# The second batch of a strided-attention and softplus kernel: one TensorE visit a pair, masks added by VectorE, and another order for the first chunk

## The chip, the cores and the metric

The kernel runs on one core of a Trainium2 chip. A core has TensorE (PE, matrix products; its weight loads are listed as PEld), VectorE (DVE), ScalarE (ACT), GpSimd (POOL) and SyncE (SP, which issues most transfers). Each engine works through its own queue in order and waits on semaphores for the others. The metric is device time in microseconds, as the median of several runs; lower is better.

## The reference

```
scores = scale * q @ k^T                      # 8 batches, 8 heads, 576 positions, 64 per head
heads 0 to 3: keep 0 <= i - j < 32            # local
heads 4 to 7: keep i >= j with i % 32 == j % 32   # strided
attn = softmax(masked scores);  x = attn @ v  # x becomes 4608 rows of 512
h = x @ w_in                                  # 512 -> 2048
g = max(h, 0) + log1p(exp(-|h|))              # softplus
out = g @ w_out                               # 2048 -> 512
```

Everything is float32 in the result. The kernel keeps that accuracy by splitting each operand of the large products into a high and a low part and adding three products: high by high, high by low, low by high.

## The kernel before, in words

Two heads make a pair, so each batch has four pairs, numbered `n` from 0 to 31 over the batches; with 8 batches, pairs 0 to 3 are batch 0 and 4 to 7 are batch 1. For strided heads the positions are regrouped by class, so that both kinds of mask leave only 64 keys to a block of 32 queries. A pair's scores then fill 9 chunks of 64 columns: `part` 0 holds six of them and `part` 1 three.

The feed-forward part runs over 9 chunks `c` of 512 rows, each in 16 steps `f` over the hidden width. A step `F` (`hidden`, 12 products of 512 columns into a `ph` bank, of which there are two) makes the hidden values; ScalarE turns them into `u` in three activations (`A`, `Ae`, `Al`), VectorE finishes the softplus (`u`), its high and low halves (`Gh`, `Gl`) are made, and a step `O` (`output`, 12 products) adds them to four `py` banks.

The attention of a pair has these steps, named by a letter and the pair: `q`, `k`, `v` (loads), `D` (lays the queries out for both heads, one half each), `S` (scores), `X` (maxima), `x` or `s` (scales the maxima into a bias), `E` (exponentials, with their sums), `r` and `R` (guard and reciprocal), `M` (normalizes), then the transposition of the probabilities: `T` on TensorE with a copy `C` for batch 0, `P` on VectorE for later ones (16 instructions in a block). `V` makes the weighted sums in two halves, and `H` and `L` put their high and low parts into `x`. The weights pass through `w` (load), `a` (ScalarE), `B` and `d` (VectorE), `h` and `l` (high and low half), for `i` and `o`, 16 tiles each, all during the first chunk.

Two things set the order. For the first chunk it is written out by hand: the string `FIRST` lists some 550 steps, and the lists `ON_POOL`, `ON_VECTOR` and `ON_SCALAR` move single steps from their usual engine. From the second chunk on a small planner (`Plan`, lines 79 to 115) places the steps from given costs and due times. In that planned part one visit of TensorE makes both score parts of pair `n` and the sums of pair `n-1`:

```
        def work(i=i, n=n):
            scores(n, 0)
            scores(n, 1)
            if joint(i):
                sums_of(n - 1)
```

The scores there carry no mask when they leave TensorE; VectorE adds it on the way to SBUF (`add_mask`). In batches 0 and 1 TensorE itself adds the mask, as a product of an identity with the mask table (`add` in `scores`, line 340). In batch 1 the score parts are separate steps `S40`, `S41` and so on, and each half of the sums is one too (`V40`, `V41`). The dictionary `shared` keeps the `po` bank whose upper columns hold part 1 of a pair's scores, and whose lower ones later take a half of the sums of the pair before. In batch 0 both halves of the sums use the one `po` bank, except for pair 3. The wait for a bank to come free is set by the `H` and `L` that read it.

`zeros(n)` clears the query buffer's unused blocks: for pairs 0 to 3 and for the buffer `qT` that all later pairs share.

Of the kernel before, what the change touches and what calls it, by code (L numbers as in the profile page):

```python
# [18 lines left out]
P = 128  # L19
# [13 lines left out]


FIRST = """
W mask q0 D00 k0 D01 S00 X00 Y00 q1 D11 S01 X01 E00 x01 Z00 k1 D10 S11 X11 q2 D20 Y11 E01 r0 wi0
S10 X10 D21 x10 k2 S21 ai0 wo0 q3 D31 S20 R0 M0 E10 Bi0 di0 X21 hi0 E11 T00 x21 C00 ao0 Z11 r1
X20 T01 C01 Bo0 D30 v0 R1 do0 V00 H00 T02 C02 L00 Y20 M1 k3 S31 X31 E21 E20 Z20 V01 li0 wi1
S30 H01 L01 ai1 Bi1 r2 di1 x31 R2 M2 wi3 ai3 T10 C10 T11 C11 v1 T12 ho0 lo0 Bi3 V10 T21 X30 Y30
di3 C12 H10 L10 V11 E30 T20 E31 Z30 C21 H11 v2 L11 r3 R3 M3 C20 T22 wi2 ai2 Bi2 V20 C22  # L40
H20 L20 di2 hi3 li3 T32 k4 wo1 C32 wi9 T31 ao1 T30 C31 v3 C30 hi1 li1 V21 H21 wo2 ao2 L21 V31 wi4
V30 Bo1 Bo2 ai9 H31 L31 Fa0 q4 H30 L30 F0 wi10 do1 Bi9 di9 wo3 Fa1 hi2 li2 D4 S40 A0
Ae0 Al0 ho1 lo1 ao3 F1 u0 Gh0 X40 x40 F2 Bo3 Gl0 ai4 Bi4 hi9 li9 di4 do2 ho2 v4 A1 E40 S41
X41 x41 wi5 ai5 q5 Bi5 Ae1 Al1 u1 wo15 D5 lo2 O0 wi6 hi4 di5 li4 F3 Gh1 Gl1 O1 A2 Ae2 wi8 ai8
do3 ai10 k5 E41 S50 r4 hi5 wo12 Bi8 li5 Al2 A3 di8 u2 R4 Ae3 M4 Al3 wi7 ai7 wi12 hi8 X50
x50 F4 u3 Gh3 Bi10 di10 F5 Gh2 Gl2 wo5 wo4 ho3 lo3 E50 P4 O2 A4 Gl3 q6 hi10 ao5 Bo5 Ae4 Al4
u4 wi11 S51 A5 Ae5 li8 X51 li10 ai6 Al5 Bi7 di7 V40 H40 x51 Gh4 Gl4 E51 r5 F8 hi7 do5 u5 ao4
L40 O3 D6 Bi6 A8 Ae8 Al8 wi14 V41 H41 Bo4 li7 di6 do4 ho4 hi6 R5 M5 k6 wo6 lo4 Gh5 S60
u8 Gh8 X60 F7 ao6 ho5 x60 E60 Gl5 li6 F6 A6 O4 ai11 L41 P5 wo7 ao7 wo8 Gl8 A7 Bo6 do6 Bo7 Ae6 Al6
v5 V50 H50 S61 Ae7 Al7 lo5 O5 ho6 u6 Gh6 Bi11 L50 do7 X61 x61 ai12 Bi12 F9 lo6 q7 wo9 D7 Gl6  # L50
V51 di12 E61 di11 H51 L51 ho7 k7 S70 X70 u7 lo7 hi11 li11 r6 k8 A9 O6 ao9 Bo9 x70
Gh7 Ae9 Gl7 ao8 F11 do9 Bo8 do8 Al9 u9 wi13 ai13 Bi13 di13 hi12 li12 wi15 ho8 lo8 wo10
ao10 Bo10 O7 R6 M6 A11 do10 hi13 F10 O8 ho10 Ae11 Al11 Gh9 u11 Gh11 ho9 lo9 F12 Gl9 O9
lo10 P6 wo11 A10 Ae10 Al10 u10 ao11 Bo11 ao12 E70 S71 ai15 do11 Bi15 v6 V60 q8 Gl11 A12 Ae12
li13 F13 Gh10 H60 X71 L60 ai14 Bo12 V61 k9 Gl10 wo14 di15 H61 Al12 do12 L61 u12 Bi14 O10 wo13
ho11 lo11 di14 A13 Ae13 Al13 u13 Qa0 x71 E71 r7 hi14 R7 O11 li14 Gh13 F14 ho12 lo12 Gh12
Gl12 O12 Gl13 A14 Ae14 Al14 M7 P7 u14 hi15 li15 ao13 Bo13 ao14 do13 ao15 v7 V70 ho13 H70 F15
A15 L70 V71 H71 lo13 Bo14 do14 ho14 lo14 O13 Ae15 L71 v8 Al15 u15 Gh15 Q1 Gh14 Gl14 O14 Bo15
do15 D8 Q0 QA1 Gl15 Qu1 QA0 Qu0 ho15 lo15 O15 Qh0 y0 Ob15 q9 y1 Qh1 Ql0 y2 y3 Ql1
"""  # L60

ON_POOL = """
D10 D20 x10 D31 hi0 x21 r2 x31 r3 hi3 hi1 ho1 Gh0 ho2 x41 hi4 r4 x50 x51 x60 Gh6 x61 r6 ho8 ho10
ho9 x71 r7 hi14 hi15 ho13 ho14 ho15
""".split()
ON_VECTOR = """
D01 M0 C00 M3 li3 li1 li2 lo1 Gl0 li9 lo2 li4 Gl1 Gl4 li6 lo6 Gl6 lo7 Gl7 li12 lo8 M6 Gl9 lo11
li14 M7 lo13 Gl14 Gl15
""".split()
ON_SCALAR = """  # L70
y1 y3
""".split()

WIDE = """
# [44 lines left out]
def attention_softplus_ffn(  # L119
# [95 lines left out]
    taken = []  # L215
    phs, us, ghs, gls = {}, {}, {}, {}

    def zeros(n):

        for h in range(2):  # L220
            to = blocks_of(n)[64 - 64 * h : P - 64 * h, :, h]
            (nc.vector if n < 2 else nc.gpsimd).memset(to, 0.0)
        if n < NPAIR:
            nc.gpsimd.memset(k_of(n)[:, :PAD], 0.0)

# [95 lines left out]

    def scores(n, part):

        b = order[n][0]
        masked = b < 2
        if b == 0:
            ps = py[2 * (n % 2) + part]
        elif b == 1 or part == 0:
            taken.append(n)
            ps = ps_s.tile([P, 512], F32, tag="ps", name=f"ps_{n}_{part}")  # L330
        else:
            shared[n] = ps_o.tile([P, 512], F32, tag="po", name=f"po_{n}")
# [14 lines left out]


        if masked and n > 0:
            add(True)  # L350
        for x in range(lo, hi):
            for place in range(2):
                a, i = block_at(x, place)
                c = TILE * a + 32 * i
                nc.tensor.matmul(  # L355
                    ps[rows[place], 64 * (x - lo) : 64 * (x - lo) + 64],
                    lhsT=blocks_of(n)[:, c // 32].rearrange("p h l -> p (h l)"),
                    rhs=k_of(n)[:, c : c + 64],
                    start=not masked or n == 0 and x == lo,
                    stop=not masked or n > 0 and x == hi - 1,  # L360
                )
        if masked and n == 0:
            add(False)
# [65 lines left out]
    def row_exp(n):  # L429
        pv, _, _ = parts(n)  # L430
        nc.scalar.activation(pv, pv, AF.Exp, scale=SCALE)

    def row_sums(n):
        pv, _, (_, sm, _, _) = parts(n)
        nc.vector.tensor_reduce(sm, pv, axis=AX.X, op=ALU.add)
# [72 lines left out]
    def weighted(n, half, joint=False):  # L508


        if joint:
            if half == 0:
                po = shared[n + 1]
            else:
                po = ps_h.tile([P, 512], F32, tag="ph", name=f"pv_{n}")
        elif half == 1 and (n == NPAIR - 1 or n >= 2 * NPAIR):
            taken.append(n)
            po = ps_s.tile([P, 512], F32, tag="ps", name=f"pv_{n}_{half}")
        else:
            po = ps_o.tile([P, 512], F32, tag="po", name=f"pv_{n}_{half}")  # L520
        pos[n, half] = po
        for x in range(NTILE // 2):
            a = NTILE // 2 * half + x
            for h in range(2):
                nc.tensor.matmul(  # L525
                    po[64 * h : 64 * h + 64, TILE * x : TILE * x + TILE],
                    lhsT=vs[n][:, a, h, :],
                    rhs=pt_of(n, a)[:, h, a % 2],
                    start=True,
                    stop=True,  # L530
                )
# [170 lines left out]
    def of(name, usual):  # L702
# [3 lines left out]
                return engine  # L706
        return usual

    first["mask"] = lambda: nc.scalar.dma_start(mask_b, masks)
    first["W"] = lambda: dummies(10)  # L710
    for n in range(2 * NPAIR + 2):
        task(f"q{n}", load_q, n)
        task(f"k{n}", load_k, n)
        if n > 2 * NPAIR:
            continue
        task(f"v{n}", load_v, n)
        if n < NPAIR:
            for h in range(2):
                task(f"D{n}{h}", lay_out_q, n, (h,), of(f"D{n}{h}", nc.scalar))
        else:  # L720
            task(f"D{n}", lay_out_q, n)
        if n >= 2 * NPAIR:
            continue
        for j in range(2):
            task(f"S{n}{j}", scores, n, j)
            task(f"X{n}{j}", maxima, n, j)
            if f"{n}{j}" in WIDE:
                task(f"Y{n}{j}", subtract, n, j)
                task(f"E{n}{j}", wide_exp, n, j)
                task(f"Z{n}{j}", sums, n, j)  # L730
            else:
                task(f"x{n}{j}", bias_of, n, j, of(f"x{n}{j}", nc.vector))
                task(f"E{n}{j}", exponentials, n, j)
# [3 lines left out]
        if f"P{n}" in FIRST.split():  # L737
            task(f"P{n}", prob_transposes, n)
        else:
            for g in range(3):  # L740
                task(f"T{n}{g}", early_transposes, n, g)
                task(f"C{n}{g}", early_copy, n, g, of(f"C{n}{g}", nc.scalar))
        for half in range(2):
            task(f"V{n}{half}", weighted, n, half)
# [255 lines left out]
```

## Time and profile before

| | us |
|---|---|
| median of 3 runs | 890.61 (890.55 to 891.92) |
| span of the profiled execution | 890.1 |
| TensorE busy | 879.0 |
| VectorE busy | 576.6 |
| ScalarE busy | 445.8 |
| GpSimd busy | 64.0 |

The page gives the profiled execution by its span from the first to the last instruction; the span is 0.5 below the median of the runs. Groups are named by line, engine, operation, and output and input tile. L629 and L669 are the products of `F` and `O`; L355 are the scores, L340 the mask products, L525 the sums, L495 and L477 the transposes on TensorE. L641, L644 and L646 are the three activations of a step, L650, L662 and L264 its softplus and halves (L264 is the line of every plain copy). A table by stretch gives, for each stretch of the span, the busy time of every engine and the number of its instructions.

### The profile page before, as it was taken

The page shows a single profiled execution, that of the slowest core. Times are in us where ns is not written, and L with a number is a line of the kernel's source. Part 1 is how long each engine was busy: PE and PEld are TensorE (multiplying, and loading weights), DVE is VectorE, ACT ScalarE, POOL GpSimd, SP SyncE. Part 2 cuts the span into 40 slices and gives each one's busy share as a digit, 9 for nine tenths or more (in the row PEclk, how much of TensorE's full clock was granted, in tenths as well). Part 3 has the DMA queues.
Part 4 walks back from the last instruction along what each step waited for, and adds up shares of the span by engine and source line. Part 5 has one row for each costly group of instructions (what it writes and reads, how often), then busy time and mean ns, then how long its engine had stood idle before and what let it go on. Part 6 is the DMA issues. An engine that isn't in the chain of part 4 may idle for free.

```text
span 890.1 us, 14332 instructions
## 1 busy us (share of the span) xinstructions
PE 879.0 (99%) x5634; PEld 723.6 (81%) x5634; DVE 576.6 (65%) x1268; ACT 445.8 (50%) x796; POOL 64.0 (7%) x93
## 2 busy tenths in 40 slices
PE   7999999999999999999999999999999999999998
PEld 5778888888888888888888888888888888888886
DVE  7878877788766777776766676677777333333332
ACT  7999665554544445445445454445543333333332
POOL 7254350000000000000000000000000000000000
PEclk9999999999999999999999999999999999999999
DMA  9856202121211122111211121111200010001001
GB/s 337 314 205 209 93 18 76 56 75 45 91 37 30 36 74 62 44 45 32 92 44 45 44 92 30 30 43 54 81 18 18 1 48 1 0 1 48 1 1 48
DMA packets 50083, 58.27 MB, mean 65 GB/s; under 512 B 3168, under 2 KB 35296, under 8 KB 50016
## 3 DMA queue, kind: packets, MB, share of 16 engines
q1 hardware_dynamic: 49728, 57.03, 19.5%
q8 instruction: 44, 0.72, 0.3%
q10 hardware_dynamic: 288, 0.33, 0.1%
q14 instruction: 23, 0.19, 0.1%
HBM read 47.91 MB, written 9.44 MB: 64 GB/s over the span
## 4 chain that ended last, share of the span: by engine, by line
PE 96%; ACT 2%; DMA 1%; DVE 1%; issue 0%; ACTq 0%
PE py L669 44%; PE ph L629 44%; PE ps L355 3%; PE pv L525 2%; PE po L525 1%; PE po L355 1%; DMA kT<-in_qk_dram 1%; PE idle L692 0%; ACT early_l L399 0%; ACT early_h L264 0%; ACT a_i L589 0%; ACT x_h L563 0%; ACT early_l L264 0%; PE py L355 0%; PE ps L340 0%
## 5 line engine op out<-in xcount | busy, mean ns | idle before, releaser
L669 PE MATMUL py<-w_o,gh 128*128 128x512 f32 x1152 | 358.4, 392 | 0.0
L629 PE MATMUL ph<-x_h,w_i 128*128 128x512 f32 x1152 | 355.5, 390 | 0.0
L641 ACT ACTIVATE u<-ph 128x512 f32<-128x512 f32 x144 | 86.3, 599 | 399.0 <-PE ph L629 398.6
L629 PEld LDWEIGHTS ph<-x_h,w_i 128*128 128x128 f32 x1152 | 215.7, 188 | 45.2
L669 PEld LDWEIGHTS py<-w_o,gh 128*128 128x128 f32 x1152 | 213.9, 188 | 46.4
L669 PE MATMUL py<-w_o,gl 128*128 128x512 f32 x576 | 224.1, 389 | 0.0
L629 PE MATMUL ph<-x_l,w_i 128*128 128x512 f32 x576 | 224.1, 389 | 0.0
L650 DVE SCALAR_TENSOR_TENSOR u<-ph,u 128x512 f32<-128x512 f32 x144 | 99.3, 690 | 178.3 <-ACT u L646 176.3
L457 DVE STREAM_TRANSPOSE pt<-prob 32x192 f32<-32x192 f32 x448 | 137.1, 314 | 6.4
L669 PEld LDWEIGHTS py<-w_o,gl 128*128 128x128 f32 x576 | 108.1, 188 | 22.8
L629 PEld LDWEIGHTS ph<-x_l,w_i 128*128 128x128 f32 x576 | 108.2, 188 | 22.6
L662 DVE TENSOR_TENSOR gl<-u,gh 128x512 fp32r<-128x512 f32 x136 | 94.3, 694 | 12.8 <-ACT gh L264 2.2
L644 ACT ACTIVATE u<-u 128x512 f32<-128x512 f32 x144 | 91.3, 634 | 4.3
L646 ACT ACTIVATE u<-u 128x512 f32<-128x512 f32 x144 | 91.1, 633 | 4.4
L264 ACT COPY qT<-prob 64x576 f32<-64x576 f32 x56 | 70.6, 1261 | 0.3
L264 DVE CAST gh<-u 128x512 fp32r<-128x512 f32 x128 | 54.5, 426 | 10.9 <-DVE u L650 0.5
L416 DVE TENSOR_TENSOR prob<-ps,mask_b 128x384 f32<-128x384 f32 x24 | 13.4, 558 | 50.0 <-PE ps L355 50.0
L355 PEld LDWEIGHTS ps<-kT,qT 128*64 128x64 f32 x720 | 24.0, 137 | 9.0 <-issue 8.5
L355 PE MATMUL ps<-kT,qT 128*64 128x64 f32 x720 | 27.6, 225 | 0.3 <-DMA kT<-in_qk_dram 0.3
L561 DVE TENSOR_TENSOR x_l<-pv,x_h 128x288 fp32r<-128x288 f32 (+2 forms) x47 | 18.8, 412 | 9.0 <-ACT x_h L563 8.9
L447 DVE TENSOR_TENSOR prob<-prob,st 128x576 f32<-128x576 f32 x27 | 21.9, 811 | 0.9
L525 PE MATMUL pv<-pt,v_in 128*64 128x96 f32 x396 | 22.1, 248 | 0.0
(100 smaller groups left out, 481.7 us busy)
## 6 DMA issues: line engine op xcount, KB each, us to landing
v_in<-in_v_dram SPq DMA_DIRECT2D x28, 320.0 KB, 3.5
out_dram<-o SPq DMA_DIRECT2D x35, 256.0 KB, 2.2
ri<-in_moe_w_in_dram SPq DMA_DIRECT2D x16, 512.0 KB, 7.3
ro<-in_moe_w_out_dram SPq DMA_DIRECT2D x16, 512.0 KB, 7.7
kT<-in_qk_dram SPq DMA_DIRECT2D x28, 288.0 KB, 2.9
prob<-in_qk_dram SPq DMA_DIRECT2D x28, 288.0 KB, 2.7
v_in<-in_v_dram SPq DMA_DIRECT2D x28, 48.0 KB, 2.7
room<-in_v_dram SPq DMA_DIRECT2D x4, 320.0 KB, 6.6
```

Source lines behind the costliest of these rows:

```text
L264: (engine.copy if engine is nc.scalar else engine.tensor_copy)(dst, src)
L355: nc.tensor.matmul(ps[rows[place], 64 * (x - lo) : 64 * (x - lo) + 64], lhsT=blocks_of(n)[:, c // 32].rearrange("p h l -> p (h l)"), rhs=k ...
L447: engine.tensor_tensor(pv, pv, rc.unsqueeze(2).broadcast_to(pv.shape), op=ALU.mult)
L457: nc.vector.transpose(pt[32 * (i + c) : 32 * (i + c) + 32, h, a : a + hi - lo, 32 * i : 32 * i + 32,], src[:, lo:hi, 32 * c : 32 * c + 32],)
L525: nc.tensor.matmul(po[64 * h : 64 * h + 64, TILE * x : TILE * x + TILE], lhsT=vs[n][:, a, h, :], rhs=pt_of(n, a)[:, h, a % 2], start=True, ...
L629: nc.tensor.matmul(ph, lhsT=w32["i", f][:, half, cc * P : (cc + 1) * P], rhs=x_of(x, cc)[:, t0 : t0 + n], start=(i == 0), stop=(i == 3 * N ...
L641: nc.scalar.activation(us[c, f], phs[c, f], AF.Abs)
L644: nc.scalar.activation(u, u, AF.Exp, scale=-1.0)
L646: nc.scalar.activation(u, u, AF.Ln, bias=1.0)
L650: nc.vector.scalar_tensor_tensor(u, in0=phs.pop((c, f)), scalar=0.0, in1=u, op0=ALU.max, op1=ALU.add)
L662: engine.tensor_tensor(g, us.pop((c, f)), ghs[c, f].bitcast(F32), op=ALU.subtract)
L669: nc.tensor.matmul(py[t], lhsT=g[:, sl], rhs=w32["o", f][:, half], start=(f == 0 and n == 0), stop=(f == NFC - 1 and n == 2),)
```

## The change

Five edits. In batch 1, a new step `J` replaces `S` and `V`: one TensorE visit makes both score parts of pair `n` and, for `n` over 4, both halves of the sums of pair `n-1`; pair 7's sums remain steps of their own, `V70` and `V71`. The masks of batch 1 are added by VectorE (`Y`, `add_mask`), one maximum over both parts (`X4`) replaces two, and one row of nine exponentials (`row_exponentials`) reads SBUF, where two steps read PSUM. In batch 0 the second half of every pair's sums goes to the `ps` bank. The clearing of `qT` becomes a step of its own (`z4`), and the layouts of batch 1 are split by head, so that either half can go to another engine. `FIRST` and the engine lists are replaced as a whole.

```diff
-    def zeros(n):
+    def zeros(n, engine):
...
-    for n in range(NPAIR + 1):
-        zeros(n)
+    for n in range(NPAIR):
+        zeros(n, nc.vector if n < 2 else nc.gpsimd)
...
     def scores(n, part):
-        b = order[n][0]
-        masked = b < 2
-        if b == 0:
+        masked = n < NPAIR
+        if masked:
             ps = py[2 * (n % 2) + part]
-        elif b == 1 or part == 0:
+        elif part == 0:
...
+    def row_exponentials(n):
+        pv, _, (mx, sm, _, _) = parts(n)
+        for a in range(NCHK):
+            nc.scalar.activation(
+                pv[:, a], pv[:, a], AF.Exp,
+                bias=mx[:, a : a + 1], scale=SCALE,
+                accum_out=sm[:, a : a + 1],
+            )
...
-        elif half == 1 and (n == NPAIR - 1 or n >= 2 * NPAIR):
+        elif half == 1 and (n < NPAIR or n >= 2 * NPAIR - 1):
             taken.append(n)
             po = ps_s.tile([P, 512], F32, tag="ps", name=f"pv_{n}_{half}")
...
+    def joint_scores(n):
+        scores(n, 0)
+        scores(n, 1)
+        if n > NPAIR:
+            for half in range(2):
+                weighted(n - 1, half, True)
...
+    task("z4", zeros, NPAIR, of("z4", nc.gpsimd))
...
+            task(f"J{n}", joint_scores, n)
+            for j in range(2):
+                task(f"Y{n}{j}", add_mask, n, j)
+            task(f"X{n}", row_maxima, n)
+            task(f"s{n}", bias_of, n, None, of(f"s{n}", nc.vector))
+            task(f"E{n}", row_exponentials, n)
```

The steps of TensorE in the two orders, from the first feed-forward step to the end of the first chunk:

```
before: Fa0 F0 Fa1 S40 F1 F2 S41 O0 F3 O1 S50 F4 F5 O2 S51 V40 F8 O3 V41 S60 F7 F6 O4 V50 S61 O5 F9
        V51 S70 O6 F11 O7 F10 O8 F12 O9 S71 V60 F13 V61 O10 Qa0 O11 F14 O12 V70 F15 V71 O13 Q1 O14 Q0 O15 Ob15
after:  Fa0 F0 Fa1 J4 F1 F2 O0 F3 F5 O1 F4 O2 J5 F8 F9 O4 O3 F7 F6 O5 O8 J6 F11 F10 O6 O7 O9 F14 F12 O10
        J7 F15 O11 F13 O14 O12 V70 V71 Qa0 Q1 O13 Q0 Ob15 O15
```

(`Fa` and `Qa` are the first nine products of a step, `F0`, `F1` and `Q0` then its last three; `Q` is a step of the second chunk.) Ahead of `Fa0` both orders run batch 0's attention: eight score steps, twelve transposition steps and eight halves of sums, in another sequence. The new lists put these steps on another engine than before, counted over the whole of `FIRST`:

| step | before | after |
|---|---|---|
| `Gh` | 14 ScalarE, 2 GpSimd | 7 ScalarE, 5 VectorE, 4 GpSimd |
| `hi`, `ho` | 18 ScalarE, 14 GpSimd | 13 ScalarE, 8 VectorE, 11 GpSimd |
| `li`, `lo` | 17 GpSimd, 15 VectorE | 17 GpSimd, 15 VectorE |
| `D` of batch 1, halves | 8 ScalarE | 2 ScalarE, 2 VectorE, 4 GpSimd |
| `C` | 11 ScalarE, 1 VectorE | 7 ScalarE, 5 VectorE |

On SyncE's queue the four pairs' `q` and `k`, and `k4`, go ahead of the first weight tile, which stood behind `q2` before.

More of the change, by code (lines that the diff above doesn't have):

```diff
@@ L35 @@
 FIRST = """
[L36 to L59, printed above, removed]
+q0 W q1 D00 D10 k0 q2 mask D20 D01 S00 S01 D11 X00 Y00 k1 q3 S10 k2 k4 k3 X01 x01 z4 S11 E00 D21
@@ new lines @@
+X10 S20 E01 Z00 x10 r0 S21 wi0 R0 X11 D31 E10 M0 wo0 Y11 E11 T01 X20 X21 Z11 D30 v0 T00 ai0 Y20 C01
+x21 C00 S30 T02 r1 R1 v1 E20 M1 ao0 Z20 E21 r2 C02 X30 S31 V00 H00 Y30 wo2 X31 T10 E30 T11 V01 Bi0
+x31 Bo0 wi1 C10 R2 L00 C11 T12 V10 H01 Z30 v2 E31 di0 v3 C12 M2 H10 T21 L01 r3 C21 wi2 R3 M3 hi0
+T20 L10 C20 li0 ao2 V11 T22 do0 wi3 H11 V20 T31 ai1 C22 H20 L11 wo3 C31 L20 Bo2 ho0 Bi1 T30 V21 C30
+T32 H21 q4 wo1 L21 C32 di1 V30 V31 ai2 do2 Bi2 H31 hi1 H30 L31 wi5 Fa0 ho2 lo0 li1 di2 v4 L30 F0
+ai3 wi4 wi6 D41 wo9 Fa1 hi2 D40 ao1 A0 J4 Ae0 li2 Al0 Bo1 Bi3 u0 di3 ai5 F1 do1 hi3 A1 F2 Gh0 Bi5
```

68 lines of the change are left out of this document (44 added, 24 removed).

## The prediction

> **What bounds the kernel now.** I read the page first, then the busy times by stretch, then the chain of waits of the first 40 us, then TensorE's timeline. The page:
>
> ```profile
> span 890.1 us, 14332 instructions
> PE 879.0 (99%) x5634; PEld 723.6 (81%) x5634; DVE 576.6 (65%) x1268; ACT 445.8 (50%) x796; POOL 64.0 (7%) x93
> PE 96%; ACT 2%; DMA 1%; DVE 1%; issue 0%; ACTq 0%
> ```
>
> TensorE is busy 99% and carries 96% of the chain. So time comes only from instructions TensorE no longer runs or from stretches in which it idles. Where it idles, by stretch (columns: stretch, length, busy of PE, PEld, DVE, ACT, POOL, clock, DMA share, GB/s):
>
> ```profile
> 0.00:30.44 30.44, 23.49 (x482) 18.29 (x483) 24.21 (x52) 24.39 (x67) 19.18 (x46) 1.00 0.90 309
> 30.44:139.60 109.16, 108.91 (x678) 87.44 (x676) 86.10 (x186) 89.39 (x205) 44.86 (x47) 1.00 0.46 158
> 139.60:696.50 556.90, 556.90 (x3623) 461.31 (x3623) 400.43 (x920) 264.38 (x414) 0.00 (x0) 1.00 0.16 51
> ```
>
> 30.44 is the first feed-forward product (step Fa0), 139.60 the first score visit of the planned part. Ahead of 30.44 TensorE idles 6.95 us; from there to 139.60 it idles 0.25, and in the next 557 us not at all. The diff touches only what runs in the first two rows; the planner's code behind them is unchanged, so I put all that follows at no change. The clock is 1.00 everywhere and plays no part.
>
> What holds the first row? The chain of waits (start, length, what):
>
> ```profile
> 9.71 1.00 ACT early_l L399 x6
> ...
> 24.11 0.38 ACT x_h L563
> 24.52 0.46 DVE x_l L561
> ```
>
> From 9.71 to 24.5 the chain is ScalarE's, instruction behind instruction, and no other engine comes in for more than a few hundredths. ScalarE is the start's bound, not the DMA.
>
> **The change, part by part.**
>
> *1. The start.* Counted in the two written orders, ahead of Fa0 ScalarE loses four copies of transposed probabilities (VectorE has five of the twelve there after the change, one before), three weight scalings (`a`) and one query layout; it gains one weight cast and one `H`. Rows:
>
> ```profile
> L264 ACT COPY pt<-pt 128x384 f32<-128x384 f32 x5 | 2.4, 475 | 0.3 <-PE pt L495 0.3
> L589 ACT ACTIVATE a_i<-ri 128x512 f32<-128x512 f32 x16 | 10.6, 676 | 0.0
> L264 ACT COPY qT<-prob 64x576 f32<-64x576 f32 x12 | 15.2, 1264 | 0.1
> L264 ACT CAST gh<-u 128x512 fp32r<-128x512 f32 x14 | 8.3, 616 | 1.1 <-DVE u L650 1.1
> 20.15 0.84 ACT L264 COPY early_l<-pt 128x384 f32<-128x384 f32 x2
> PE pv L525 <- DVE x_l L561: 1.3, 3, 0.5
> ```
>
> 4 x 0.475 + 3 x 0.676 + 1.264 - 0.616 - 0.4 = 4.2 us less; two copies in a row take 0.84, not 0.95, so each instruction of a full queue costs about 0.1 less than its length, and the net six fewer give 3.6 us. The last row is TensorE's waits for the `L` steps that free the one bank of the sums; with the second half in the other bank they go, 1.3 us, but ScalarE is the later party, so I count 3.6 and not 4.9. What is late next: TensorE itself, whose floor is 1.18 (first start) + 23.49 = 24.7, so at most 5.8 us come. VectorE is busy 24.21 in this stretch and its own load falls slightly, so it does not hold Fa0 above 27. The moved DMAs: the first weight tile goes behind four more loads of 288 KB, which at the 309 GB/s of the row is 3.8 us; scaling, cast and halves of that tile stand far ahead of Fa0 in the order, so nothing (3.8 at most if that lead were gone). The two memsets of `z4` go behind GpSimd's prologue and still ahead of its first layout: nothing. I take 3.6, Fa0 at 26.8; ends 0.5 (the chain re-forms on waits between engines, as the 6 us in which ScalarE idles now suggest) and 5.8.
>
> *2. TensorE's visits in the second batch.* A visit is an excursion from the 512-wide products to 64-wide instructions. Rows of TensorE's timeline (start, length, ...):
>
> ```profile
> 30.44 0.73 PE L629 MATMUL ph<-x_h,w_i 128*128 128x512 f32 x2
> ...
> 35.11 0.39 PE L629 MATMUL ph<-x_l,w_i 128*128 128x512 f32 x1
> 36.99 0.40 PE L629 MATMUL ph<-x_l,w_i 128*128 128x512 f32 x1
> ...
> 44.16 0.62 PE L629 MATMUL ph<-x_h,w_i 128*128 128x512 f32 x2
> 44.84 0.62 PE L629 MATMUL ph<-x_h,w_i 128*128 128x512 f32 x2
> ...
> 106.76 0.39 PE L629 MATMUL ph<-x_l,w_i 128*128 128x512 f32 x1
> 108.29 0.40 PE L669 MATMUL py<-w_o,gl 128*128 128x512 f32 x1
> ...
> 139.34 0.39 PE L629 MATMUL ph<-x_l,w_i 128*128 128x512 f32 x1
> 141.43 0.40 PE L669 MATMUL py<-w_o,gl 128*128 128x512 f32 x1
> 157.09 0.39 PE L629 MATMUL ph<-x_l,w_i 128*128 128x512 f32 x1
> 160.17 0.39 PE L669 MATMUL py<-w_o,gl 128*128 128x512 f32 x1
> 696.75 0.39 PE L629 MATMUL ph<-x_l,w_i 128*128 128x512 f32 x1
> 698.79 0.40 PE L669 MATMUL py<-w_o,gl 128*128 128x512 f32 x1
> ```
>
> Three products take 0.68 (44.16 to 44.84), 0.2267 each. A visit costs the time from the start of the last product before it to the start of the third behind it, less 0.68: a masked part-0 score 1.20 (35.11 to 36.99), one half of sums 0.85, an unmasked score of both parts 1.41 (139.34), the joint visit 2.40 (157.09), both halves of sums together 1.36 (696.75). The order now has 11 visits among the steps: S40, S41, S50, S51+V40, V41+S60, V50+S61, V51+S70, S71+V60, V61, V70, V71. Their sum: from 30.44 to the end of the product at 139.34 are 109.13 us and 35 steps of 12 products, 420 x 0.2267 = 95.2, so 13.9. The changed order has J4 without sums, J5, J6, J7 joint, and V70 next to V71: 1.41 + 3 x 2.40 + 1.36 = 10.0. The difference, 3.9, has some tenths of product jitter in it; I take 3.6. The 16 mask products go with it, and the 0.25 of idle time. This is the surest term, since all three prices stand in the same trace; ends 3.2 and 3.9.
>
> *3. What VectorE gets for it.* After Fa0, counted in the orders: 13 casts (5 Gh, 3 hi, 5 ho), 2 more low halves, the layouts D40 and D41, 8 mask adds, one more `B` and `d`. One maximum over both parts replaces two: nothing.
>
> ```profile
> 30.44:50.00 19.56, 19.56 (x141) 15.55 (x139) 14.79 (x28) 19.31 (x44) 4.55 (x8) 1.00 0.96 348
> L264 DVE CAST gh<-u 128x512 fp32r<-128x512 f32 x4 | 1.6, 424 | 0.2
> L615 DVE TENSOR_TENSOR w_o<-a_o,w_o 128x512 fp32r<-128x512 f32 x7 | 5.5, 791 | 0.4 <-POOL w_o L264 0.4
> L615 DVE TENSOR_TENSOR w_o<-a_o,w_o x7: 678/684/1433, 34.3 to 123.2; 128x512 fp32r<-128x512 f32 x7
> L264 DVE COPY early_h<-raw_q 64x576 f32<-64x576 f32 x1 | 0.9, 902 | 0.3 <-DMA raw_q<-in_qk_dram 0.3
> L416 DVE TENSOR_TENSOR prob<-ps,mask_b 128x384 f32<-128x384 f32 x1 | 0.6, 558 | 1.6 <-PE ps L355 1.6
> L416 DVE TENSOR_TENSOR prob<-po,mask_b 128x192 f32<-128x192 f32 x1 | 0.3, 349 | 0.0
> L600 DVE SCALAR_TENSOR_TENSOR a_o<-ro,a_o 128x512 uint32<-128x512 uint32 x15 | 10.3, 690 | 0.2
> L615 POOL TENSOR_TENSOR w_o<-a_o,w_o x9: 1287/1297/1813, 22.2 to 131.7; 128x512 fp32r<-128x512 f32 x9
> L447 POOL TENSOR_TENSOR prob<-prob,st x2: 1151/1152/1153, 49.8 to 65.7; 128x576 f32<-128x576 f32 x2
> 52.35 5.10 DVE L457 STREAM_TRANSPOSE pt<-prob 32x192 f32<-32x192 f32 x16
> DVE u L650 <- ACT u L646: 9.3, 7, 2.4
> ```
>
> 13 x 0.42 + 2 x 0.68 + 2 x 0.90 + 4 x 0.91 + 1.1 = 13.4 us. So VectorE goes from 86.1 busy in 109.2 to 99.5 in 105.6 (109.2 - 3.6), 94%. ScalarE loses 13 casts (8.1) and six half layouts (7.6) and gains three scalings (2.0): 89.4 to 75.7. GpSimd gets four half layouts and stays near half busy. VectorE becomes the fullest helper, with 6.1 us left over. What hides it is the order's own slack: weights are made several steps ahead, and each step's `u` has the two banks of `ph`. Without that cover all of what passes 105.6 is lost one for one. A full helper need not stall TensorE: ScalarE was busy 19.31 of the 19.56 us behind Fa0, and TensorE idled in none of them.
>
> The tightest place is the last pair: J7 to V70 has only five steps of 2.72 and the visit's 2.4 on TensorE, 16.0. The chain in it: scores 1.3, then VectorE's eight instructions from Y70 to s7 (two mask adds 0.91, three of 0.69, three shorter: about 4.4, an estimate), nine exponentials at 1.00 for three (2.9, by the chain's row), guard and reciprocal 0.6, the normalization 1.15 on GpSimd, the transposes 5.10: 15.5. A VectorE more than half a microsecond behind shows as a stall there. Behind `q4`, VectorE stands in its queue for D41 and D40, and with it `hi2`; J4 then waits at most about 1 us. I take 0.8 us of stalls in all; ends 0 and 4.
>
> **Sum.** -3.6 - 3.6 + 0.8 = -6.4 on a span of 890.1. The median of the runs shown is 890.61, 0.5 over this span; 890.6 - 6.4 = 884.2.
>
> **A rule against it.** The seven low halves of VectorE range from 0.68 to 1.43, and the long ones fall where GpSimd works on its own. The Trainium skill, SBUF — State Buffer, section "Who interferes with whom", says that a VectorE instruction with two SBUF inputs and a GpSimd instruction that reads SBUF exclude each other for a whole instruction. The trace agrees in kind, by those 1.43; how much of it, the second rival works out from rows.
>
> **The rivals.**
> *The start is not ScalarE's to give.* Against it the unbroken ScalarE chain; for it the 6 us in which ScalarE idles ahead of 30.44. Gain 0.5 there: 887.3. Chance 0.12.
> *VectorE held by GpSimd.* After Fa0 VectorE runs some 55 instructions with two SBUF inputs (28 `d`, 15 low halves, the `Gl` and the normalizations). GpSimd is then busy about half the time; if each met one of its instructions half the time and waited half of its 1.30, that were 55 x 0.5 x 0.65 = 18 us. Now the same count for 27 `d` and 13 low halves is 40 x 0.41 (44.86 of 109.16) x 0.65 = 10.7, and the rows show about 2: 0.11 over the minimum for each low half, 0.01 for each `d`. So the trace bears out a fifth, some 3.5 us of the 18. In full, VectorE needs 99.5 + 14.5 = 114 in 105.6 and TensorE stalls 8.4: 891.8. I give half to all of it 0.10 (887.5 to 891.8).
> *VectorE as the bound (slower).* If its waits stay at today's 23.1 us (109.2 - 86.1), it needs 99.5 + 23.1 = 122.6, TensorE stalls 17: 900.4. It decides from 13.3 us of remaining waits on, where both gains are eaten. Against it: 9.3 us of them are waits for ScalarE's last activation of a step, which comes earlier with 13.7 us less work on ScalarE, and no TensorE time hung on them. Chance 0.07.
> *Everything fits.* TensorE at its floor in the start, no stall: 890.6 - 5.8 - 3.6 = 881.2. Chance 0.08.
>
> **Chances.** My forecast, 882.5 to 886.5, has 0.63. A difference under 0.2% (1.8 us) can hardly be told from none. Faster: 0.63 + 0.12 + 0.08 and a little of the second rival, 0.84; within 0.2%: 0.09; slower: 0.07. The range 881.0 to 889.0 leaves out the slow rival, the worse half of the second and a remnant below.
>
> **What would show it.** First product at 26 to 28 us; visits in the first chunk of 1.41, three of 2.40, one of 1.36, and no mask product behind the first batch; ScalarE's busy time between 30 and 136 near 76, VectorE's near 99; pieces of TensorE idle behind V70 or a `ph` product released by VectorE summing to about 0.8. The forecast is wrong if Fa0 stays near 30, or if TensorE's idle time after Fa0 passes 4 us.

## The result, and the profile after

The changed kernel takes 907.07 us (906.64 to 907.55), the kernel before, on the same chip, 891.26 (890.55 to 891.98): a ratio of 1.0172, 95% interval 1.0158 to 1.0187. It is 1.7% slower where 0.7% faster was forecast. From the page of the changed kernel, in the order of the page shown before:

```profile
span 905.8 us, 14294 instructions
PE 880.6 (97%) x5618; PEld 724.0 (80%) x5618; DVE 597.9 (66%) x1290; ACT 431.7 (48%) x772; POOL 75.5 (8%) x95
PE 86%; DVE 7%; DMA 2%; ACT 2%; issue 1%; SPq 1%; POOL 0%; DVEq 0%; ACTq 0%; POOLq 0%
L639 PE MATMUL ph<-x_h,w_i 128*128 128x512 f32 x1152 | 357.5, 391 | 9.5 <-DVE u L660 5.8
```

VectorE carried 1% of the chain before and carries 7% now. The table by stretch of the changed kernel, cut at its first feed-forward product and at the first visit of the planned part (the columns are those of the table before):

```profile
0.00:30.37 30.37, 22.94 (x483) 18.95 (x483) 20.71 (x49) 20.18 (x58) 18.43 (x45) 0.89 0.78 268
30.37:155.27 124.90, 111.06 (x662) 87.32 (x660) 110.92 (x212) 79.46 (x189) 57.07 (x50) 0.99 0.43 151
155.27:712.00 556.73, 556.73 (x3623) 460.99 (x3622) 400.42 (x920) 264.37 (x414) 0.00 (x0) 1.00 0.17 50
```

The start lasts as long as before (30.37 and 30.44). The planned part is the same (556.73 and 556.90). All the loss is in the middle: 124.90 against 109.16, 15.7 us. The 420 products of that stretch are 95.2 us and the five visits at the forecast's prices 10.0, so 19.7 us are stalls; before, TensorE idled 0.25 us there, and the forecast had 0.8. The profile counts only 13.8 of them as idle time (124.90 less the busy 111.06): the record of a product lasts 0.39 us though the next one can follow after 0.23, so each of its 16 waits hides its first 0.16, and seven products ran at half the clock (last section). The two come to about 4 of the other 5.9 us. What the profile shows as waits of TensorE, from 26 to 160 us:

```profile
PE ph L639 <- DVE u L660: 5.8, 5, 1.5
PE ph L639 <- DVE x_l L571: 3.9, 4, 1.2
PE ps L352 <- POOL qT L262: 1.0, 2, 0.6
PE py L679 <- POOL gl L672: 0.9, 1, 0.9
PE ph L639 <- DVE w_i L625: 0.9, 1, 0.9
```

Measured as in the prediction, the visits are J4 1.41, J5 4.12, J6 5.07, J7 4.83 and V70 with V71 1.36. The first and the last are at their price. The three joint ones are 1.7 to 2.7 us over the 2.40.

**Two things that the traces show side by side.** The first is in the start. The mask table is loaded from ScalarE's queue. Before, that transfer was the second step of the order; the new order lists it behind two query layouts (`q0 W q1 D00 D10 k0 q2 mask`). One row of the timeline before, then three of the timeline after (start, length, engine, what, and in brackets the idle time with what ended it):

```profile
0.76 0.39 ACTq L709 DMA_DIRECT2D mask_b<-in_masks_dram  x1
```

```profile
3.58 1.27 ACT L262 COPY early_h<-raw_q 64x576 f32<-64x576 f32 x1 [1.20 <-DMA raw_q<-in_qk_dram]
4.36 0.38 ACTq L727 DMA_DIRECT2D mask_b<-in_masks_dram  x1
11.02 0.53 PE L337 MATMUL py<-mask_b,ident_b 128*64 128x384 bf16 x2 [3.52 <-DMA mask_b<-in_masks_dram]
```

The load goes out 3.6 us later, behind a layout that waits for its own data, and TensorE waits 3.52 us for it. Behind that wait the granted clock is 0.51 from 8 to 15 us, which is why the table has 0.89 for the start where it had 1.00 before.

The second is behind the first product. The groups by form from there to the planned part, the changed kernel first, then the kernel before (instructions, busy us, mean ns):

```profile
L610 DVE SCALAR_TENSOR_TENSOR a_i<-ri,a_i 128x512 uint32<-128x512 uint32 x14 | 13.4, 966 | 0.0
L610 DVE SCALAR_TENSOR_TENSOR a_o<-ro,a_o 128x512 uint32<-128x512 uint32 x15 | 13.1, 880 | 0.1
L672 DVE TENSOR_TENSOR gl<-u,gh 128x512 fp32r<-128x512 f32 x10 | 10.1, 1018 | 0.8 <-ACT gh L262 0.8
L603 DVE TENSOR_SCALAR a_i<-a_i 128x512 uint32<-128x512 uint32 x14 | 8.9, 654 | 0.1
L625 POOL TENSOR_TENSOR w_i<-a_i,w_i 128x512 fp32r<-128x512 f32 x11 | 16.7, 1514 | 7.7 <-DVE w_i L262 4.4 <-ACT w_i L262 3.1
```

```profile
L600 DVE SCALAR_TENSOR_TENSOR a_i<-ri,a_i 128x512 uint32<-128x512 uint32 x12 | 8.4, 711 | 0.2
L662 DVE TENSOR_TENSOR gl<-u,gh 128x512 fp32r<-128x512 f32 x10 | 7.1, 717 | 2.2 <-ACT gh L264 2.2
L593 DVE TENSOR_SCALAR a_i<-a_i 128x512 uint32<-128x512 uint32 x12 | 5.3, 439 | 0.4 <-ACT a_i L589 0.4
L615 POOL TENSOR_TENSOR w_i<-a_i,w_i 128x512 fp32r<-128x512 f32 x7 | 9.3, 1332 | 7.8 <-DMA ri<-in_moe_w_in_dram 5.0 <-ACT w_i L264 2.7
```

The same instruction on the same tile takes 0.97 us in the mean instead of 0.71, because some of them take up to 1.8. Below, "excess" is the sum over all instructions of a stretch of their length over the shortest of the same form in the run, where that is over 0.1 us. VectorE's excess was 3.8 us in 8 of 186 instructions, and is 19.6 in 26 of 211; GpSimd's went from 3.3 to 8.6. Each of these 8 and of these 26 overlaps an instruction of GpSimd. Two of the long ones in the changed kernel's timeline, each with the GpSimd instruction beside it:

```profile
31.54 1.78 POOL L625 TENSOR_TENSOR w_i<-a_i,w_i 128x512 fp32r<-128x512 f32 x1 [3.07 <-ACT w_i L262]
32.09 1.78 DVE L610 SCALAR_TENSOR_TENSOR a_i<-ri,a_i 128x512 uint32<-128x512 uint32 x1
...
65.29 1.74 POOL L625 TENSOR_TENSOR w_i<-a_i,w_i 128x512 fp32r<-128x512 f32 x1
65.79 1.79 DVE L672 TENSOR_TENSOR gl<-u,gh 128x512 fp32r<-128x512 f32 x1
```

Where TensorE stalls, VectorE has been running without a pause. The chain of waits around J5 (start, length, what), and the product that stands at its end in the timeline:

```profile
54.58 1.52 DVE prob L457
...
56.13 0.37 DVE pt L467
...
61.27 0.69 DVE u L660
...
63.48 0.68 DVE u L660
```

```profile
64.22 0.73 PE L639 MATMUL ph<-x_h,w_i 128*128 128x512 f32 x2 [1.49 <-DVE u L660]
```

From the stretched normalization (1.52, where the shortest of its form takes 0.76) through sixteen transpositions to the `u` that frees the `ph` bank, VectorE is the chain for 9.6 us. In the five stretches of 20 us from 30 to 130 it is busy 18.4 to 19.4 of 20; before, over its whole middle stretch, 79%.

### The profile page after: what moved, and what is told of

Read it like the earlier page. It is cut to its first block, busy times and chain, and to the rows that moved or that the text cites. A ratio compares the mean times of both kernels' runs of the same rounds, so it can differ in the third digit from the quotient of the medians.

```text
span 905.8 us, 14294 instructions
## 1 busy us (share of the span) xinstructions
PE 880.6 (97%) x5618; PEld 724.0 (80%) x5618; DVE 597.9 (66%) x1290; ACT 431.7 (48%) x772; POOL 75.5 (8%) x95
## 4 chain that ended last, share of the span: by engine, by line
PE 86%; DVE 7%; DMA 2%; ACT 2%; issue 1%; SPq 1%; POOL 0%; DVEq 0%; ACTq 0%; POOLq 0%
PE py L679 40%; PE ph L639 39%; PE ps L352 2%; PE pv L535 2%; DVE pt L467 2%; PE po L535 1%; DMA ri<-in_moe_w_in_dram 1%; PE po L352 1%; DVE a_i L610 1%; DVE gl L672 1%; DMA mask_b<-in_masks_dram 1%; DVE u L660 1%; DVE a_o L610 0%; PE pt L505 0%; DVE a_i L603 0%
## 5 line engine op out<-in xcount | busy, mean ns | idle before, releaser
L672 DVE TENSOR_TENSOR gl<-u,gh 128x512 fp32r<-128x512 f32 x136 | 97.3, 716 | 11.7 <-ACT gh L262 0.8
L262 ACT COPY qT<-prob 64x576 f32<-64x576 f32 x50 | 63.0, 1259 | 3.2 <-DMA prob<-in_qk_dram 2.9
L262 DVE CAST gh<-u 128x512 fp32r<-128x512 f32 x133 | 56.6, 426 | 10.9 <-PE py L679 0.5
L413 DVE TENSOR_TENSOR prob<-ps,mask_b 128x384 f32<-128x384 f32 x28 | 15.6, 556 | 49.2 <-PE ps L352 49.2
L352 PEld LDWEIGHTS ps<-kT,qT 128*64 128x64 f32 x672 | 21.9, 137 | 11.0 <-issue 9.2
L352 PE MATMUL ps<-kT,qT 128*64 128x64 f32 x672 | 25.7, 226 | 1.0 <-POOL qT L262 1.0
L573 ACT CAST x_h<-pv 128x288 fp32r<-128x288 f32 (+2 forms) x44 | 15.7, 370 | 15.8 <-PE pv L535 15.6
L413 DVE TENSOR_TENSOR prob<-po,mask_b 128x192 f32<-128x192 f32 x28 | 10.0, 356 | 19.5 <-ACT x_h L573 19.5
```

What stands on the lines that cost most here:

```text
L262: (engine.copy if engine is nc.scalar else engine.tensor_copy)(dst, src)
L352: nc.tensor.matmul(ps[rows[place], 64 * (x - lo) : 64 * (x - lo) + 64], lhsT=blocks_of(n)[:, c // 32].rearrange("p h l -> p (h l)"), rhs=k ...
L413: nc.vector.tensor_tensor(pv, sv, m, op=ALU.add)
L672: engine.tensor_tensor(g, us.pop((c, f)), ghs[c, f].bitcast(F32), op=ALU.subtract)
```

## The experiments

My theory was: the late mask costs about 3 us, and the long instructions, VectorE and GpSimd excluding each other, most of the rest. The rivals: VectorE simply has too much work, so that anything taken off it helps; the joint visit itself does not fit the chunk; or the small steps of the attention's chain stand in the wrong place of GpSimd's queue. Times are compared by the ratio to the kernel before, run in turn on the same chip (0.1% is 0.9 us).

**mask_first.** The changed kernel with the mask load as the first step.

```diff
-q0 W q1 D00 D10 k0 q2 mask D20 D01 S00 S01
+mask q0 W q1 D00 D10 k0 q2 D20 D01 S00 S01
```

> The changed kernel with one step moved: the load of the mask table stands first in the written order again, as it did before the change; now it stands behind two query layouts on ScalarE's queue, and TensorE's first mask product waits 3.5 us for it. Theory (two separate losses: the late mask costs the start, VectorE is the bound behind it): the first product comes at 26 to 27 us instead of 30.4, and because VectorE works without a pause from 12 us on, all of it moves forward with it: 902.5 to 904. TensorE still idles 12 to 15 us between the first product and V70. Rival (one loss: the late mask set VectorE back, and that is what makes it late all through the first chunk): most of the 16 us return, under 895. Rival (VectorE's load alone sets the end of the first chunk): no gain over 1 us, 906 or more.

903.83 us, ratio 1.0133 (1.0118 to 1.0148); the first product at 27.73 instead of 30.37. By stretch:

```profile
0.00:27.73 27.73, 21.45 (x483) 17.29 (x483) 21.73 (x49) 19.97 (x58) 17.88 (x45) 1.00 0.88 294
27.73:151.50 123.77, 109.91 (x662) 86.44 (x660) 110.90 (x212) 79.71 (x189) 57.07 (x50) 1.00 0.44 152
```

The late mask costs 3.5 us by the ratios: some 2.6 in the start, where the clock is now 1.00, and 1.1 in the middle, where the stretch at half the clock is gone. The rest of the new start does bring 2.7 us. The middle keeps its 19.6 us of excess, so that is another matter.

**late_mask.** The reverse: the kernel before with the mask load behind two layouts, for which `q1` and `D11` go ahead of it.

```diff
-W mask q0 D00 k0 D01 S00 X00 Y00 q1 D11 S01
+W q0 D00 k0 D01 q1 D11 mask S00 X00 Y00 S01
```

> The kernel before, with the mask load put behind the first two query layouts on ScalarE's queue, as the changed kernel has it (with q1 and its layout brought ahead of it). Theory: the mask lands at 9 to 11 us instead of about 4.5, the first scores' mask product waits 3 to 4 us, and the chain of ScalarE behind it moves with it: first product at 33.5 to 35 and 893.5 to 895.5. Rival (ScalarE and VectorE catch up by doing weights in the wait): under 892.

897.33 us, ratio 1.0060 (1.0045 to 1.0075): 5.4 us slower, the first product at 35.36, both more than forecast. TensorE's waits in it name the mask, and from 8 to 16 us the granted clock is 0.57:

```profile
PE py L338 <- DMA mask_b<-in_masks_dram: 6.2, 1, 6.2
```

The place of this load is worth microseconds in either order.

**bank.** The kernel before with only the second bank for batch 0's sums.

```diff
-        elif half == 1 and (n == NPAIR - 1 or n >= 2 * NPAIR):
+        elif half == 1 and (n < NPAIR or n >= 2 * NPAIR):
```

> One part of the change alone: in the first batch the second half of every pair's sums goes to the other bank; all else as before the change. Theory (ScalarE is the later party in the start): the waits of TensorE for L go, the first product comes 0 to 0.5 us earlier, 890.1 to 890.7. Rival (these waits stand on the chain): 1.3 us earlier, 889.3.

892.14 us, ratio 1.0004 (0.9994 to 1.0013). The bank alone brings nothing, as the prediction had it.

**joint_old.** Joint visits and VectorE's masks in the order and with the lists of the kernel before (of the order, TensorE's steps up to `F8`).

```diff
-Fa0 F0 Fa1 S40 F1 F2 S41 O0 F3 O1 S50 F4 F5 O2 S51 V40 F8
+Fa0 F0 Fa1 F1 F2 J4 O0 F3 O1 F4 F5 O2 J5 F8
```

> One part of the change alone: one TensorE visit a pair, masks by VectorE and a single maximum in the second batch, in the order and with the engine lists of the kernel before (J at the place of the second score part; the sums, v5, v6, u7, L41 and H50 moved as little as that needs); all other parts as before the change. Theory (the visits are worth what their rows say, and VectorE at some 82% busy hides its mask adds): 886.5 to 888, visits of 1.41, 2.40 and 1.36. Rival (the joint visit needs more at once, sums transposed and two banks free, and stalls for it): visits of 3 to 5 us as in the changed kernel, 890 or more.

915.24 us, ratio 1.0257 (1.0240 to 1.0274). The visits, measured as before, are 1.4, 9.3, 6.1 and 5.9 us. TensorE's waits after 25 us:

```profile
PE ph L638 <- DVE u L659: 8.6, 3, 6.4
PE ph L638 <- DVE x_l L570: 3.4, 1, 3.4
```

My forecast for it, 887, fell. The excess is only 2.4 us here, so this loss is not the exclusion. The longest wait, 6.4 us, comes behind J5, whose own instructions ran without a pause: the product that follows waits for a `u`, and in VectorE's queue that `u` stands behind the guard `r5`, which waits 2.6 us for ScalarE's exponentials of the same pair. So here it is the order, written for separate steps, that does not fit; the other waits were not followed.

**pool_writes.** `mask_first` with GpSimd's low halves as memsets, as long, which read nothing.

```diff
+        if engine is nc.gpsimd:
+            for _ in range(3):
+                engine.memset(t[:, 1].bitcast(F32), 0.0)
+            return
```

> The changed kernel with the mask load first, in which GpSimd's low halves (li, lo and Gl on its list) are replaced by three clearings of the same tile: about as long on GpSimd, but they read nothing. The low parts it would have made are left out, so this is an experiment on time alone. Theory (VectorE is held while GpSimd reads SBUF: 26 of its 211 instructions of the first chunk are long now, 19.6 us over their minimum): the two-input instructions d, Gl and low halves fall to 0.68 to 0.70, the excess from 19.6 to 4 to 8 us (copies, casts and B can still be held), TensorE's waits fall by as much as 10 us and the time to 890 to 896. Rival (VectorE's number of instructions is the bound and the long ones only fill its waits): the time stays within 2 us of 903.8 although the excess falls. Rival (GpSimd's mere presence holds VectorE, reading or writing): excess and time stay.

896.55 us, ratio 1.0050 (1.0035 to 1.0065), 7.4 us under `mask_first`. Its middle stretch, and the first of the groups by form:

```profile
27.66:144.05 116.39, 109.68 (x661) 87.89 (x660) 100.50 (x211) 79.44 (x189) 60.12 (x97) 0.99 0.44 160
```

```profile
L610 DVE SCALAR_TENSOR_TENSOR a_i<-ri,a_i 128x512 uint32<-128x512 uint32 x14 | 10.2, 735 | 0.0
L628 POOL MEMSET w_i<- 128x512 f32 x32 | 18.2, 570 | 2.7 <-ACT w_o L262 1.3
```

GpSimd is busy about as long as before (60.1 and 57.1) and the order is the same. VectorE's instructions are the same too, yet they take 10.4 us less, with an excess of 9.7 instead of 19.6 (forecast 4 to 8, and 890 to 896 for the time). By kind: VectorE's instructions with two SBUF inputs fall from 14.7 us of excess, in 21 of them, to 4.6 in 9, and each of these 9 overlaps one of GpSimd's remaining instructions that read; none is long beside memsets alone. VectorE's casts, copies and `tensor_scalar`, with one input, stay at 5 us (4.9 and 5.0), and 11 of them are long beside memsets alone. So GpSimd's reading lengthens the two-input instructions, and its writing is enough for the others. The 7.4 us of time are the most that the reading is worth: the memsets also wait for no input, so GpSimd runs earlier in its queue (it idles 0.9 us ahead of its `Gl` steps instead of 8.5). TensorE waited only 0.9 us for GpSimd's `Gl` in `mask_first`, and `chain_off_pool` below speaks against a large part of that kind.

**pool_short.** `mask_first` with each low half and each cast of GpSimd as one memset of 0.5 us (the edit of the low halves is shown, that of the casts is alike).

```diff
+        if engine is nc.gpsimd:
+            engine.memset(t[:, 1].bitcast(F32), 0.0)
+            return
```

> The changed kernel with the mask load first, in which every low half and every weight or g cast of GpSimd is one clearing of its tile (0.45 us, reads nothing); the values that GpSimd would have made there are left out, so this is on time alone. VectorE's and ScalarE's work and the order are the changed kernel's. Theory (the time behind the first product is lost to the lock and to GpSimd's lateness that follows, not to the order's visits or to VectorE's load): excess of VectorE under 6 us, joint visits near 2.40, time 885 to 891. Rival (VectorE's load and its waits in an order this tight cost the rest): excess falls as well, but the time stays at 893 to 897, with VectorE still the one TensorE waits for.

891.06 us, ratio 0.9993 (0.9984 to 1.0003), 12.5 us under `mask_first`. Its middle stretch, and four rows of its timeline ahead of J6:

```profile
26.69:139.16 112.47, 108.81 (x662) 88.12 (x660) 95.16 (x212) 78.82 (x189) 30.74 (x50) 0.98 0.47 168
```

```profile
61.59 0.75 DVE L418 TENSOR_REDUCE st<-prob 128x9 f32<-128x576 f32 x1
...
65.78 0.69 POOL L622 MEMSET w_o<- 128x512 f32 x1 [3.47 <-DVE a_o L610]
66.55 0.50 POOL L390 TENSOR_SCALAR st<-st 128x9 f32<-128x9 f32 x1
67.08 0.35 ACT L434 ACTIVATE prob<-prob,st 128x64 f32<-128x64 f32 x1 [0.54 <-POOL st L390]
```

The first product comes 1.0 us earlier; the excess behind it is 3.3 us, and 7.3 us of stalls are left of the 18.6 in `mask_first` (stretch less 95.2 and 10.0). J6 alone keeps 3.2 of them, and half the clock behind it costs about 1 more: the maxima of pair 5 are ready at 62.3, but their scaling stands in GpSimd's queue behind a cast that waits for VectorE's `a_o`, and the exponentials begin 4.7 us later. Of the 5.1 us between this run and `pool_writes`, the runs do not tell how much is the exclusion by GpSimd's casts and how much its shorter queue.

**casts_act** and **all_casts.** `mask_first` with VectorE's 13 casts on ScalarE, and then GpSimd's 15 as well.

```diff
-... hi2 D40 lo2 li3 Gh1 Gh2 hi4 Gl2 M4 Gl5 ho4 lo4
+... D40 lo2 li3 Gl2 M4 Gl5 lo4
```

> The changed kernel with the mask load first and the 13 casts that it gave to VectorE (Gh, hi, ho) back on ScalarE; order and GpSimd as they are. VectorE loses 13 x 0.42 = 5.5 us. Theory of the lock: the excess of VectorE stays at 15 to 20 us and the time falls by at most those 5.5: 898 to 901. Rival (the load given to VectorE is the bound): 5.5 us and more return, as the waits shrink with it: under 897. Rival (ScalarE, put behind E in its queue, becomes late): 903 or more.

> As before, and the 15 casts on GpSimd go to ScalarE too. ScalarE rises from 79 to about 95 us behind the first product, GpSimd falls by 10. Theory of the lock: of the 26 long VectorE instructions a quarter goes (GpSimd busy 57 to 47), 3 to 5 us less than the run with 13 casts moved: 894 to 898. Rival (ScalarE's queue becomes the bound): not faster than that run.

904.04 us, ratio 1.0134 (1.0118 to 1.0151), and 905.51, 1.0151 (1.0133 to 1.0168); excess 18.0 and 15.6. Both are slower than forecast. The middle stretch of the first, and a wait of VectorE in it that `mask_first` does not have:

```profile
27.30:151.03 123.73, 109.78 (x662) 86.46 (x660) 105.30 (x199) 85.80 (x202) 56.26 (x50) 1.00 0.43 152
```

```profile
DVE w_o L624 <- ACT w_o L261: 3.4, 2, 2.3
```

VectorE is busy 5.6 us less and the stretch is as long as before, to 0.1 us. So taking work off VectorE does not help by itself. That its load is harmless is not shown: 904 is what was expected if the casts come late on ScalarE, and VectorE now waits 3.4 us for some of them.

**no_pool_low.** `casts_act` with all of GpSimd's low halves after the start on VectorE.

```diff
-li14 lo9 lo10 M6 lo11 Gl12 Gl14 li13 lo15 Gl13 lo13 y2
+li14 lo9 lo10 M6 lo11 Gl12 Gl14 li13 lo15 Gl13 lo13 y2 li1 li2 Gl0 lo1 ...
```

> The changed kernel with the mask load first, VectorE's 13 casts back on ScalarE and all 24 low halves of GpSimd behind Fa0 on VectorE. VectorE gets 24 x 0.61 = 14.6 us more work and loses 5.5; GpSimd keeps casts, layouts and small steps. Theory of the lock: the excess falls from 19.6 to under 6 us, so that VectorE's busy time falls although it has 9 us more to do (110.9 to about 105), and the time is 892 to 900. Rival (load is the bound): VectorE has 9 us more, so the time rises, 908 or more.

909.39 us, ratio 1.0196 (1.0179 to 1.0213). Its middle stretch, and the second of TensorE's waits in it:

```profile
26.66:156.07 129.41, 113.88 (x661) 90.39 (x660) 107.46 (x222) 86.10 (x202) 20.77 (x26) 0.95 0.41 145
```

```profile
PE py L679 <- DVE gl L672: 5.8, 2, 5.6
```

The excess is down to 5.4 us, VectorE is busy 3.4 us less than in `mask_first`, and the kernel is slower. The forecast of 892 to 900 fell, and the time is the one expected if VectorE's load were the bound. The low halves moved to VectorE stand where the order put them for another engine; one `Gl` comes 5.6 us late. The run does not separate VectorE's load from the place of these steps in its queue. What it shows is that taking the exclusion away in this way buys nothing.

**lists_only.** The order before with the engine lists of the change.

```diff
-D10 D20 x10 D31 hi0 x21 r2 x31 r3 hi3 hi1 ho1 Gh0 ho2 ...
+D21 x10 r0 D31 D30 r1 r2 x31 r3 hi0 hi3 Gh0 ho1 ho3 ...
```

> The kernel before, its order and its separate score and sum steps kept, with the changed kernel's engine lists for all steps that both have (casts, low halves, copies, batch 0's layouts, scalings, guards, normalizations). Theory (which engine does a step makes the collisions): excess of VectorE behind the first product 10 us or more instead of 3.8, time 895 or more. Rival (the order makes them: the same instructions at other times): excess under 7 us, time 889 to 893.

919.61 us, ratio 1.0327 (1.0294 to 1.0359), the first product at 36.43, an excess of 16.7 us in 24 instructions. With the old lists the excess was 3.8 in the old order and 2.4 in `joint_old`. So in the old order it comes with the lists, not with the joint visits; the new order with the old lists was not run.

**chain_off_pool.** `mask_first` with the small steps of batch 1's chain, and two normalizations, on VectorE.

```diff
-... Gh0 ho1 s4 ho3 r4 D51 hi9 Gh5 ho5 ho7 s5 r5 D60 ...
+... Gh0 ho1 ho3 D51 hi9 Gh5 ho5 ho7 D60 ...
```

> The changed kernel with the mask load first, and the small steps of the second batch's chain (s4, s5, r4 to r7, M5, M7) on VectorE instead of GpSimd. GpSimd's low halves, casts and layouts stay, and so does most of the lock. Theory (the lock is the larger part): excess of VectorE stays at 15 us or more, the time falls by 0 to 4 us, 900 to 904. Rival (the pair's chain is late because its small steps queue on GpSimd behind casts that wait for weights): joint visits come down to about 2.4 each and the time falls by 6 us or more, under 898.

905.11 us, ratio 1.0146 (1.0130 to 1.0161), excess 18.0; forecast 900 to 904. The place in GpSimd's queue that cost J6 its time in `pool_short` is not what costs while the exclusion stands.

**start_only**, **start_late** and **start_d4.** Could the new start serve the old second batch? The start of `mask_first` with the second bank, then the rest of the order before; then with `F0` ahead of the weight steps that were left over; then with pair 4's layout ahead of them too.

```diff
 start_only: ... wi5 ai3 lo0 Bi3 di3 di2 hi3 li3 wi9 ao1 li1 wi4 Bo1 ai9 Fa0 L30 F0 wi10 ... D4 S40
 start_late: ... wi5 Fa0 L30 F0 li1 ai3 lo0 Bi3 di3 di2 hi3 li3 wi9 ao1 wi4 Bo1 ai9 wi10 ... D4 S40
 start_d4:   ... wi5 Fa0 L30 F0 li1 D4 ai3 lo0 Bi3 di3 di2 hi3 li3 wi9 ao1 wi4 Bo1 wi10 ... S40
```

> The changed kernel's order and engines up to Fa0, with the mask load first and the second bank for the first batch's sums, and behind it the kernel before: its order, its engines, TensorE's masks and separate visits. Fourteen weight steps that the kernel before had ahead of Fa0 come behind it. Theory: first product at 27 to 28 us instead of 30.4, and with nothing else changed the gain stays: 887.5 to 889. Rival (ScalarE, 99% busy behind Fa0 before, now has these steps on top): the gain is given back as stalls in the first 20 us behind Fa0, 890 to 892.

> start_only once more, with L30 and F0 put ahead of the weight steps that had come behind Fa0 (in start_only L30 stood behind eight VectorE instructions of those steps, and TensorE waited 3.7 us for it), and li1 first among them. Everything else as there. Theory (that stall was only the place of L30): first product at 27.3, no wait over 1 us behind it, 888 to 890, faster than the kernel before. Rival (ScalarE and VectorE are short by the weight work that was not done ahead of Fa0, wherever it stands): the stall moves to F1 or F2, 891 to 896.

> start_late with the query layout of the first pair of the second batch (D4, both halves, 2.5 us) right behind the first weight low half on ScalarE's queue, and the weight scaling ai9, which there waited 2.6 us for its transfer, behind the three activations of the first step. Theory (the 6 us of that visit are D4's place in ScalarE's queue): the first score visit takes 1.2 us instead of 7.3, the first product stays at 27.2, and the time is 3 us under the kernel before, 889 (0.9965). Rival (ScalarE and VectorE are short of work done in time, and the wait only moves to the next step that they serve): another wait of TensorE of 2 to 5 us before 60 us, and a time of 892 or more (ratio 1.000 to 1.005).

896.07 us, ratio 1.0050 (1.0035 to 1.0065); 895.53, 1.0043 (1.0030 to 1.0056); 897.47, 1.0059 (1.0042 to 1.0076). The first product is at 27.3, 27.2 and 28.0. The longest wait of TensorE behind it in each of the three, in that order:

```profile
PE ph L627 <- DVE x_l L559: 3.7, 1, 3.7
```

```profile
PE ps L353 <- ACT qT L262: 4.4, 1, 4.4
```

```profile
PE ph L627 <- ACT a_i L587: 5.1, 1, 5.1
```

The stall moves from the low half of `x` to the query layout to the weights. My forecasts of a time below or at the kernel before (887.5 to 889, 888 to 890, 889) were wrong in all three, and in the last two the rival was right: in these starts the helpers have done less of the weights' work when the first product begins, and what was skipped is waited for within 10 us. None of the runs beats the kernel before.

## Why the prediction was wrong, point by point

- *Term 1, the start, -3.6.* The mechanism was right and the size nearly: with the mask in place the first product comes at 27.7, forecast 26.8. In the kernel as changed the term is 0. The step that failed is the account of moved transfers: it went through SyncE's queue, and left out the one load on ScalarE's, whose move costs 3.5 us. The chain of waits was read from 9.71 us on, and the first mask products stand ahead of that. The second bank alone counts for nothing, as expected.
- *Term 2, the visits, -3.6.* The prices hold where the operands were ready (J4 1.41, V70 with V71 1.36; 2.40 for J7 in `pool_short`). The mask products are gone. The 13.9 for the old visits was a remainder and not a sum of prices; measured one by one the eleven come to 13.4. So the saving is there, about 3.4, under the stalls.
- *Term 3, stalls, +0.8.* Measured 19.7. This is the step that failed most. It rested on "the trace bears out a fifth" of the exclusion: the rate of the old order, 2 us of 10.7, was carried over to new engine lists. The rule in full gave 18 us of excess; 19.6 were measured. That the two are so close is in part luck: the 18 counts instructions with two SBUF inputs, and these have 14.7 (21 of some 55, 0.7 each); the other 4.9 are in five `tensor_scalar` with one input, which the rule left out. `pool_writes` shows up to 7.4 us of the time to hang on GpSimd's reading, `pool_short` 12.5 on its large instructions as a whole.
- *The second rival's price.* Even in full it was put at 8.4 us of stalls and 891.8, because the excess was first laid into VectorE's spare 6 us. That is the second fault: where a `u`, an `L` or a transposition came late, TensorE waited, whatever idle time VectorE had elsewhere. VectorE still has 14.0 of 124.9 us idle.
- *VectorE's load.* Without its excess it is 110.9 - 19.6 = 91.3 us; the forecast's 99.5, less the 3.8 of excess that it took over from the kernel before, was 95.7. So it was not too low. Whether this load adds to the loss is open: `casts_act` took 5.6 off for no gain, but put it on ScalarE.
- *The slower rival* (waits stay at 23.1 us) had the sign and not the mechanism: VectorE's idle time fell to 14.0, and its instructions grew instead.
- *What stays open.* About 7 us of stalls remain without GpSimd's large instructions. In that run J6, whose scaling comes late from GpSimd's queue, and half the clock behind it account for about 4 of them, and V70 with V71, which wait for transposed probabilities, for 1.4; the rest was not isolated. How the 12.5 us divide between the exclusion and GpSimd's shorter queue is not known either. Why the old lists meet so rarely (8 instructions of 186, with GpSimd busy 41% of the stretch) was not tested either.

The ledger: 907.07 - 884.2 = 22.9 is 3.6 of start, 18.9 of stalls (19.7 - 0.8), and 0.6 by which the kernel before stood higher in that call, to within 0.3.

## What to carry to other kernels

A rate of collision between two engines belongs to one order and its engine lists: when a change replaces these, price the exclusion in full and compare lengths of the same instruction form before and after, since no wait in the profile names it. Whenever an order is rewritten, list the transfers that each engine's queue issues, the compute engines' included, and ask what stands ahead of each. A first product that comes earlier is a gain only if the work skipped for it is not awaited a few microseconds later.

## What the runs showed of the hardware

*The exclusion runs both ways and without a wait in the profile.* VectorE's instruction of 0.62 us lasts 1.78 beside GpSimd's, and GpSimd's of about 1.3 lasts up to 2.00 beside VectorE's. The Trainium skill, SBUF — State Buffer, section "Who interferes with whom", calls the ports that VectorE and GpSimd share an exclusive lock, and says of VectorE's 2-port modes that whoever issues first has them for the whole instruction and the other is blocked. The lengthened rows agree with that, also where VectorE has two inputs: in both pairs shown VectorE ends 0.55 us behind GpSimd, a little less than the 0.62 and 0.68 us that its instruction takes alone.

*The clock after an idle stretch.* In places where TensorE had idled, the products behind it came every 0.43 us instead of 0.23. Two stretches, of the changed kernel and of `start_d4` (PEclk is the number behind POOL's count):

```profile
131.20:133.80 2.60, 2.60 (x7) 1.98 (x6) 1.31 (x3) 0.92 (x6) 1.27 (x2) 0.50 0.00 0
```

```profile
40.00:45.00 5.00, 4.96 (x12) 3.80 (x12) 3.44 (x7) 4.62 (x17) 1.40 (x2) 0.50 1.06 396
```

The granted clock is 0.50 in both. In `start_d4` 5.1 us of idling came before; in the changed kernel it was two waits of 0.77 and 0.90 us with one product between them. `mask_first` has the same two waits (0.76 and 0.91), and its clock stays at 1.00, so they are not always enough; what decides, the runs do not show. The products of such a stretch cost 0.2 us each on top of the stall, some 1.4 us for seven. The forecast took the clock as 1.00 throughout. The Trainium skill, TensorE: Matmul & The Clock Gate, Part 1, gives half the clock after an idle window of about 3.4 us; `start_d4` agrees, and the changed kernel's 1.7 us of waits are less than that.
